# Retention feeding a WaveMLP block: the first half of a hand-written instruction order is written anew

## Chip, cores and metric

The kernel runs on one core of a Trainium2 chip. The metric is the time of one execution on the device in microseconds (us). All engines of a core run their own queues in order and wait for one another by semaphores: TensorE (PE), VectorE (DVE), ScalarE (ACT), GpSimd (POOL) and SyncE (SP). DMAs are issued from the queues of SyncE, ScalarE and GpSimd.

## What is computed

q, k and v have 4 batches, 8 heads, 768 steps and 64 channels. A retention with a decay per head gives x, and a gated mixing block follows on x.

```python
gamma = 1.0 - 2.0 ** (-5.0 - np.arange(H))
for t in range(S):                       # retention, scale = 1/8
    state = gamma * state + einsum('bhd,bhe->bhde', k[:, :, t], v[:, :, t])
    y[:, :, t] = scale * einsum('bhd,bhde->bhe', q[:, :, t], state)
x = y.transpose(0, 2, 1, 3).reshape(B, S, H * D)      # 4 x 768 x 512
theta = x @ w_theta
zr, zi = x * cos(theta), x * sin(theta)
u = x + einsum('ts,bsd->btd', w_tok_r, zr) + einsum('ts,bsd->btd', w_tok_i, zi)
out = u + maximum(u @ w_ch, 0.0)
```

## The kernel before

The retention is done in chunks. The work is cut into 24 *units*: unit n is one of 4 batches, one of 3 stretches of 256 steps, and one half of the heads (n even or odd). Two units of the same stretch make two blocks C of 128 steps of x; there are 24 blocks, six to a batch. Each step is a small function, and the table `ORDER` at the head of the file lists the calls of these functions one after the other. Each engine's queue gets its instructions in the order of that table; nothing reorders them afterwards. A token is a function, its arguments, and where it can run in several places, an engine: `s` SyncE's queue, `a` ScalarE, `v` VectorE, `p` GpSimd.

For unit n:

- `Lk`, `Lq`, `Lv` load 256 KB each of k, q and v (tiles `kqf`, `vf`).
- `ck` casts k to bf16 (tile `kqb`). q is cast either plainly (`cq`) or with its decay (`cqs`, a multiplication); after a plain cast the decay is put on at the end (`XA`, VectorE) instead of a plain copy (`XB`). `cv` casts v with its decay (tile `vb`).
- `Tk`, `Tq` transpose k and q on PE (four 128x128 each, into `kq_ps`), `E` copies them out (`kqT`). `Dk` does both by a DMA for some later units.
- `A` makes the scores (`at_ps`), `m` masks them (`at`, VectorE), `Y` multiplies them with v into `r_ps`.
- `ST` makes the unit's own state sum, `S0` and `S1` add the states up (`s`), `SB` casts them (`sbd`), and `I` adds the older state's share of the output.
- `XB` or `XA` gives the transposed output `xT`.

For block C: `Tx` and `Ex` (or `Dx`, a DMA) turn `xT` into `x_sb`; `Hh` multiplies `xT` with theta's weight (`th_ps`, four 512-wide matmuls); `CN` takes sine and cosine on ScalarE (`cs`); `z` multiplies them with x. The token weights come in rows: `Pw(r, g)` loads group g of the real (0) or imaginary (1) weight through GpSimd's queue; group 0 is row block 0, group 1 the blocks 1 and 2, group 2 the last three. `Tw` and `Ew` transpose a row block (six 128x128). `Pth` and `Pch` load the weights of theta and of the last product. `M(t, s)` is one of six pairs of 512-wide matmuls that make output block t; `u`, `Tu`/`Eu` or `Du`, `O`, `f`, `SO` finish and store it. `Z` is a filler: two 512-wide matmuls of zeros whose result nobody reads. There are 14 in the first half of the table and one at its end.

The constants: `const3` makes the small decays, `const9` and `const8` the large ones that `XA` needs (four activations each, `qx`), `const4` the identity, and `const7` loads ScalarE's table for the sine. DMAs on the two hardware queues share eight completion semaphores in turn, so one can be issued only when the eighth before it has landed.

Of the kernel before, what the change touches and what calls it, by code (L numbers as in the profile page):

```python
# [27 lines left out]
S0.2.v S1.2 SB.2.1.a Z.11 cqs.3.p Tq.3 Lv.3.s Tx.0 Tk.3 Z.3 ck.4.p Lv.4.s Lk.5.s Lq.5.s Lv.5.s
Lq.6.s Lk.6.s Lv.6.s Lq.7.s E.3.a SB.2.0.v I.2 Y.2 XB.2.1.a Ex.0.a cv.3.v cq.4.p Tk.4 Lq.8.s A.3
ST.3 Lk.7.s S0.3.v SB.3.0.a S1.3 Lv.7.s Lk.8.s Tx.1 Tq.4 SB.3.1.p cv.4.p m.3 Pw.1.0 XB.2.0.a Ex.1.a  # L30
I.3 Lv.8.s E.4.a cq.5.a Y.3 Pw.0.0 ST.4 Hh.0 ck.5.a S0.4.v XB.3.0.v XB.3.1.v cv.5.v CN.0.1 A.4
CN.0.0 Tq.5 Hh.1 Tk.5 SB.4.0.p SB.4.1.a Pw.0.1 Hh.2 m.4 E.5.v I.4 Y.4 ST.5 ck.6.a Tk.6 Tx.2 cq.6.a
CN.1.1 CN.1.0 XA.4.1 A.5 XA.4.0 m.5 Lq.9.s Ex.2.v S0.5.v z.0.p Tq.6 E.6.a CN.2.0 cv.6.p Hh.3
SB.5.0.v Tx.3 Tw.1.0 z.1.v SB.5.1.a Ew.1.0.v Ex.3.a CN.2.1 A.6 I.5 Y.5 ST.6 XA.5.0 z.2.v Tw.0.0
CN.3.0 Tx.4 CN.3.1 Ew.0.0.v S0.6.v XA.5.1 Ex.4.v Hh.4 CN.4.0 CN.4.1 Tw.0.1 M.0.1 Pw.1.1 z.3.v M.0.0
Tw.0.2 Pw.1.2 Ew.0.2.a SB.6.1.a Hh.5 z.4.p SB.6.0.p Lk.9.a M.0.3 ck.7.p cqs.7.p M.0.2 CN.5.1 CN.5.0
cq.8.a m.6 Ew.0.1.v Tw.1.1 Tw.1.2 Ew.1.1.v Lv.9.s M.0.4 M.1.0 Tx.5 Ew.1.2.v M.1.1 S1.6 Tk.7 M.1.4
Pch Ex.5.v z.5.v cv.7.v Tq.8 Tq.7 M.1.2 E.7.a M.0.5 I.6 Y.6 ST.7 A.7 ck.8.a u.0 S0.7.v m.7 XA.6.1
SB.7.1.a M.1.5 M.1.3 XA.6.0 Tw.1.3 M.2.5 Pw.0.2 M.2.3 u.1 S1.7 Tk.8 M.2.1 M.2.0 SB.7.0.v Ew.1.3.a
Tu.0 I.7 cv.8.p E.8.a cv.9.p Y.7 ST.8 A.8 cqs.9.v ck.9.v M.2.4 Du.1 Lk.10.s Eu.0.a XB.7.1.a XB.7.0.v  # L40
S0.8.v SB.8.0.v M.2.2 Tx.6 Tq.9 Tk.9 Lv.10.a cv.10.p ck.10.p Lq.10.s S1.8 u.2 m.8 O.0 E.9.a SB.8.1.a
Hh.6 Tw.1.4 I.8 Y.8 A.9 CN.6.0 Du.2 Lq.14.s CN.6.1 Ex.6.v f.0 ST.9 Tw.0.3 Hh.7 Ew.1.4.v Ew.0.3.a
S0.9.v Tw.0.4 M.3.0 Tw.1.5 CN.7.0 CN.7.1 M.3.2 Dx.7 M.3.1 M.3.5 M.3.3 Lv.12.s Lk.12.s Ew.1.5.v
XA.8.1 Ew.0.4.v Lq.12.s M.3.4 u.3 S1.9 Tw.0.5 Tk.10 M.4.5 cqs.10.p XA.8.0 m.9 M.4.3 Tq.10 SB.9.1.a
SB.9.0.a I.9 O.2 Lq.11.s Lk.11.s E.10.a Lk.15.s Ew.0.5.v Lk.14.s Y.9 ST.10 A.10 z.7.p Lv.11.s
# [12 lines left out]
SB.14.0.p Lv.16.s Hh.13 S1.14 u.8 Tx.12 M.10.1 cv.15.p cv.17.p SB.14.1.p M.10.0 M.10.4 cqs.18.v
M.10.5 CN.13.0 CN.13.1 Hh.12 CN.12.1 I.14 m.15 Y.14 CN.12.0 ST.15 S0.15.v XB.14.1.a SB.15.0.a M.10.3
cv.16.v Dk.16 Dk.17 Du.7 Dx.13 M.10.2 Dk.18 O.6 SB.15.1.p XB.14.0.v S1.15 I.15 Y.15 ST.16 SO.5.a  # L60
cv.18.p f.6 S0.16.v A.16 M.11.4 SB.16.1.p M.11.1 Lq.21.a Ex.12.a z.12.p SB.16.0.a Lk.19.s Lk.20.s
XB.15.0.a u.10 z.13.p XB.15.1.a m.16 O.7 Du.10 I.16 Y.16 ST.17 f.7 A.17 Tu.8 Hh.15 CN.15.1 CN.15.0
# [571 lines left out]
```

## Time and profile before

| | |
|---|---|
| time, three runs | 165.47, 165.74, 165.96 us; median 165.74 |
| span of the profiled execution, from its first to its last instruction | 164.0 us |
| PE busy | 153.7 us (94% of the span) |
| VectorE, ScalarE, GpSimd busy | 113.1, 79.6, 76.9 us |
| read from and written to HBM | 25.69 and 6.29 MB, 195 GB/s over the span |
| mean granted clock of TensorE | 0.999 |

The profiled execution's time with what lies around its span isn't given; the median of the three runs lies 1.74 us above the span. "Busy" is the time in which at least one instruction of the engine is under way, and matmuls overlap in their pipeline, so a busy PE isn't one that starts matmuls at its best rate. In the rows a name such as `kqb` is a tile's name without its buffer number, `x4` the number of instructions that a row gathers, and the brackets hold the engine's idle time before them with what ended it.

### The profile page before, as it was taken

To read this page: it belongs to the slowest core of one execution; us is meant where nothing else is said; L and a number is where in the kernel's file an instruction comes from. 1 tells how busy PE (TensorE), PEld (TensorE's weight loads), DVE (VectorE), ACT (ScalarE), POOL (GpSimd) and SP (SyncE) were. 2 spreads that over 40 slices of the span, in tenths; PEclk is the share of its full clock that TensorE was granted. 3 is DMA by queue.
4 is the path that set the end of the run, shared out by engine and by line. 5 is a ranking of instruction groups with operands and counts; after the bars stand their busy time and mean duration, and the time that the engine had idled before them with its cause. 6 is when DMAs were issued, how large, how long until landed. Compare 5 with 4: busy or idle time off the path is not lost.

```text
span 164.0 us, 4889 instructions
## 1 busy us (share of the span) xinstructions
PE 153.7 (94%) x2001; PEld 87.0 (53%) x2030; DVE 113.1 (69%) x210; ACT 79.6 (49%) x142; POOL 76.9 (47%) x109
## 2 busy tenths in 40 slices
PE   5997789999999999999999999999999999999992
PEld 1455556656666655654454565555555545455550
DVE  3298677977993896994879895789867760244462
ACT  4976889983658245762433725832341616000020
POOL 7957279186306733730307599951469104500000
PEclk9999999999999999999999999999999999999999
DMA  4999999999999999949999896999999438514455
GB/s 118 297 290 251 272 284 250 279 217 280 210 214 257 290 170 222 310 115 285 318 259 199 173 247 182 187 169 301 213 271 131 96 83 211 160 68 123 104 209 203
DMA packets 69062, 34.93 MB, mean 213 GB/s; under 512 B 26416, under 2 KB 66096, under 8 KB 69040
## 3 DMA queue, kind: packets, MB, share of 16 engines
q1 hardware_dynamic: 56032, 23.73, 67.4%
q10 hardware_dynamic: 10320, 7.47, 16.1%
q0 software_dynamic: 2688, 3.41, 12.1%
q8 instruction: 16, 0.26, 0.7%
q14 instruction: 6, 0.05, 0.1%
HBM read 25.69 MB, written 6.29 MB: 195 GB/s over the span
## 4 chain that ended last, share of the span: by engine, by line
PE 73%; DMA 12%; ACT 5%; POOL 4%; issue 2%; DVE 1%; DVEq 0%; SPq 0%; POOLq 0%; ACTq 0%
PE y_ps L509 35%; PE o_ps L536 12%; PE th_ps L469 9%; DMA row<-in_moe_w_tok_i_dram 5%; DMA kqf<-in_k_dram 4%; DMA kqf<-in_q_dram 4%; PE r_ps L423 3%; ACT qx L233 3%; PE at_ps L346 2%; PE r_ps L411 2%; PE kq_ps L316 2%; PE w_ps L491 2%; PE y_ps L561 2%; PE r_ps L373 1%; PE u_ps L521 1%
## 5 line engine op out<-in xcount | busy, mean ns | idle before, releaser
L509 PE MATMUL y_ps<-z,wti 128*128 128x512 bf16 x131 | 49.6, 379 | 1.0 <-issue 1.0
L509 PE MATMUL y_ps<-z,wtr 128*128 128x512 bf16 x131 | 49.7, 379 | 0.3
L483 POOL TENSOR_TENSOR z<-cs,x_sb 128x1024 bf16<-128x1024 bf16 x12 | 25.4, 2124 | 17.6 <-DMA x_sb<-xT 10.0
L355 DVE TENSOR_TENSOR at<-at_ps,mask 128x1024 bf16<-128x1024 f32 x24 | 29.2, 1216 | 0.6 <-PE at_ps L346 0.5
L308 POOL TENSOR_TENSOR vb<-vf,vsc 128x512 bf16<-128x512 f32 x17 | 18.0, 1063 | 21.3 <-DMA vf<-in_v_dram 21.0
L542 DVE SCALAR_TENSOR_TENSOR ot<-o_ps,u 128x512 f32<-128x512 f32 x23 | 15.8, 688 | 12.9 <-PE o_ps L536 12.8
L469 PE MATMUL th_ps<-wth,xT 128*128 128x512 bf16 x88 | 23.9, 379 | 0.5
L516 DVE TENSOR_TENSOR u<-y_ps,x_sb 128x512 bf16<-128x512 f32 x23 | 15.8, 688 | 12.0 <-PE y_ps L509 11.9
L536 PE MATMUL o_ps<-wch,uT 128*128 128x512 bf16 x88 | 23.2, 379 | 0.4 <-issue 0.2
L476 ACT ACTIVATE cs<-th_ps,zerob 128x512 bf16<-128x512 f32 x24 | 16.4, 684 | 12.7 <-PE th_ps L469 8.2
L476 ACT ACTIVATE cs<-th_ps,halfpi 128x512 bf16<-128x512 f32 x24 | 16.3, 684 | 10.5 <-issue 4.3
L139 POOL CAST sbd<-s 64x256 bf16<-64x256 f32 (+1 forms) x21 | 10.0, 476 | 22.9 <-DVE s L391 20.5
L509 PEld LDWEIGHTS <-wtr 128*128 128x128 bf16 x138 | 13.5, 98 | 12.7
L509 PEld LDWEIGHTS <-wti 128*128 128x128 bf16 x138 | 13.5, 98 | 11.9 <-DVE wti L139 0.2
L137 ACT COPY kqT<-kq_ps 128x1024 bf16<-128x1024 bf16 x12 | 12.1, 1012 | 10.9 <-PE kq_ps L316 10.9
L137 ACT CAST kqb<-kqf 128x512 bf16<-128x512 f32 x17 | 10.2, 619 | 8.0 <-DMA kqf<-in_k_dram 7.2
L469 PEld LDWEIGHTS <-xT 128*128 128x128 bf16 x96 | 8.9, 98 | 8.3
L536 PEld LDWEIGHTS <-uT 128*128 128x128 bf16 x92 | 8.4, 98 | 8.6
L316 PE MATMUL kq_ps<-ident,kqb 128*128 128x128 bf16 x120 | 11.2, 219 | 0.4 <-ACT kqb L137 0.2
L278 PE MATMUL zz<-zero 128*128 128x512 bf16 x27 | 9.5, 481 | 2.0 <-DVE zero L192 1.9
L423 PE MATMUL r_ps<-at,vb 64*64 64x128 bf16 x384 | 10.0, 221 | 1.1 <-DVE at L355 1.1
L316 PEld LDWEIGHTS <-kqb 128*128 128x128 bf16 x120 | 8.2, 98 | 4.5 <-POOL kqb L139 0.6
(77 smaller groups left out, 204.6 us busy)
## 6 DMA issues: line engine op xcount, KB each, us to landing
vf<-in_v_dram SPq DMA_DIRECT2D x20, 256.0 KB, 6.0
kqf<-in_k_dram SPq DMA_DIRECT2D x19, 256.0 KB, 5.3
kqf<-in_q_dram SPq DMA_DIRECT2D x17, 256.0 KB, 5.1
out_dram<-ot ACTq DMA_DIRECT2D x12, 256.0 KB, 3.0
out_dram<-ot SPq DMA_DIRECT2D x11, 256.0 KB, 3.1
kqf<-in_q_dram ACTq DMA_DIRECT2D x7, 256.0 KB, 5.4
kqf<-in_k_dram ACTq DMA_DIRECT2D x5, 256.0 KB, 5.0
vf<-in_v_dram ACTq DMA_DIRECT2D x4, 256.0 KB, 6.1
```

The lines of the kernel that those rows point to most:

```text
L137: nc.scalar.copy(dst, src)
L308: engines[e].tensor_mul(in_blocks(vb), by_token(raw["vf", n]), _bcast_last(K["vsc"][:, i, :, h * HU:(h + 1) * HU], D))
L316: nc.tensor.transpose(st["kq_ps", n][:, 4 * w + x, :], st["kqb", n][:, w, x * P:(x + 1) * P], K["ident"])
L355: nc.vector.tensor_mul(at.rearrange("p g j a t -> p (g j) (a t)"), st["at_ps", n].rearrange("p g j a t -> p (g j) (a t)"), _bcast_mid(K["m ...
L423: nc.tensor.matmul(st["R", n + 1][c][g * D:(g + 1) * D, j * P:(j + 1) * P], st["vb", n][rows, lo:lo + D], st["at", n][rows, g, j, a, :], s ...
L469: nc.tensor.matmul(th_ps, st["xT", C][:, j, :], K["wth"][:, j, :], start=(j == 0), stop=(j == 3))
L476: nc.scalar.activation(st["cs", C][:, w, :], st["th_ps", C], AF.Sin, bias=K["zerob" if w else "halfpi"], scale=1.0)
L483: engines[e].tensor_mul(st["z", b][:, c], st["cs", C], _bcast_mid(x_of(C), 2))
L509: nc.tensor.matmul(st["y", t], K["wT"][r][:, s0, t0 * P:(t0 + 1) * P], st["z", b][:, s0, r, :], start=(done == 0 and r == 0), stop=(done = ...
L516: nc.vector.tensor_add(st["u", t], st["y", t], st["x", b][:, t0, :])
L536: nc.tensor.matmul(o_ps, st["uT", t][:, j, :], K["wch"][:, j, :], start=(j == 0), stop=(j == nD - 1))
L542: nc.vector.scalar_tensor_tensor(st["ot", t], st["o", t], 0.0, st["u", t], ALU.max, ALU.add)
```

## The change

The first 435 of the table's 927 tokens are written in another order. From there on (at block 10's theta, about 68 us into the trace of before) the tables are equal but for one copy, `XB.12.1`, which goes from ScalarE to VectorE. The first half holds the same work: the same 49 loads of k, q and v, the same transposes, products and 14 fillers. What differs:

- the order of the loads, and their queues: 22 hardware DMAs of that half are on ScalarE's queue instead of 10;
- `Pth` stands behind the first state casts instead of behind unit 2's v cast; `Hh.0` and `Hh.1` stand ahead of `Y.3` and `ST.4`;
- five of the fillers stand ahead of `Tk.0` instead of seven;
- `cqs` on VectorE 5 times instead of 3, `cv` 4 instead of 3; `ck` on GpSimd 9 times instead of 5 and on VectorE once instead of 5; `E` on VectorE 6 times instead of 3; `Ew` on ScalarE 7 times instead of 3; `SB` on GpSimd 9 instead of 6;
- the units whose decay is put on at the end are 1, 5, 6, 7 and 8 instead of 4, 5, 6, 8 and 11.

```diff
 ORDER = """
-const2 Lv.0.s const1 const6.v Z.29 Z.2 const5 Z.38 Lk.0.a const3 Z.35 Z.8 Lq.0.s Lv.1.s Z.28 constA
-const4 Lq.1.a cqs.0.v const9 Lk.1.s cv.0.p Z.39 const8 ck.0.p Tk.0 Tq.0 ck.1.a E.0.v Lq.4.a ST.0
...
+const2 Lv.0.s const1 const6.v Z.29 Z.2 const5 Z.38 Lk.0.s constA Lk.1.a Lq.0.a Z.28 ck.0.p Z.8 const4 const3
+cqs.0.v ck.1.a Tk.0 cv.0.p Lv.2.s Lq.1.a Tq.0 Z.27 ST.0 Lv.1.s E.0.a const9 Lq.3.s Lk.3.a cv.2.p cq.1.p
...
```

The table is five lines shorter, so every line number of the kernel after is five lower (L303 for L308 and so on).

**ScalarE, the start of the program.** `kqf` are loads of k and q, `kqb` their casts, `kqT` the copy of the first transposes, `qx` the large decays, `xT` and `sbd` outputs and states. Before:

```order
L157 DMA kqf<-in_k_dram 128x4x128
L240 ACT_TABLE_LOAD
L240 ACTIVATE qsc<-arg,lscale 128x48
L240 ACTIVATE vsc<-arg,zerob 128x48
L157 DMA kqf<-in_q_dram 128x4x128
L233 ACTIVATE qx<-pos,lscale,lgp 128x512 x4
L233 ACTIVATE qx<-pos,lscale,lgp 128x256 x4
L137 CAST kqb<-kqf 128x512
```

Now:

```order
L152 DMA kqf<-in_k_dram 128x4x128
L152 DMA kqf<-in_q_dram 128x4x128
L235 ACT_TABLE_LOAD
L235 ACTIVATE qsc<-arg,lscale 128x48
L235 ACTIVATE vsc<-arg,zerob 128x48
L132 CAST kqb<-kqf 128x512
L152 DMA kqf<-in_q_dram 128x4x128
L132 COPY kqT<-kq_ps 128x1024
L228 ACTIVATE qx<-pos,lscale,lgp 128x512 x4
L152 DMA kqf<-in_k_dram 128x4x128
L152 DMA kqf<-in_q_dram 128x4x128
L152 DMA vf<-in_v_dram 128x4x128
```

The cast of unit 1's k and the copy E.0 have moved ahead of the decays, and the loads of q1, k3, q4 and v3 stand between these activations.

**GpSimd, up to theta's weight.** `ident` is the identity, `vb` a cast of v, `wth` theta's weight; the numbers tell tiles apart. Before:

```order
masks.py:199 AFFINE_SELECT ident_159<-ident_159 128x128
L308 TENSOR_TENSOR vb_174<-vf_91,vsc_131 128x512
L139 CAST kqb_166<-kqf_128 128x512
L302 TENSOR_TENSOR kqb_193<-kqf_164,qsc_130 128x512
L139 CAST sbd00_95<-s2_247 64x2x64
L308 TENSOR_TENSOR vb_253<-vf_143,vsc_131 128x512
L308 TENSOR_TENSOR vb_317<-vf_255,vsc_131 128x512
L173 DMA wth_99<-in_moe_w_theta_dram 128x4x512
L139 CAST kqb_406<-kqf_384 128x512
```

Now:

```order
L134 CAST kqb_148<-kqf_128 128x512
masks.py:197 MEMSET ident_153 128x128
masks.py:199 AFFINE_SELECT ident_153<-ident_153 128x128
L303 TENSOR_TENSOR vb_171<-vf_91,vsc_159 128x512
L303 TENSOR_TENSOR vb_214<-vf_173,vsc_159 128x512
L134 CAST kqb_164<-kqf_175 128x512
L134 CAST sbd00_95<-s2_221 64x2x64 x2
L168 DMA wth_99<-in_moe_w_theta_dram 128x4x512
L134 CAST kqb_310<-kqf_212 128x512
L134 CAST kqb_308<-kqf_290 128x512
```

The cast of k0 stands ahead of the identity; q1 is cast plainly here (`kqb_164`) and v1 no longer; behind the weight come k3 (`kqb_310`) and then k2 (`kqb_308`).

**ScalarE, the first sine and cosine.** `cs` are sine and cosine of a block. Before:

```order
L137 CAST kqb_581<-kqf_459 128x512
L137 CAST kqb_581<-kqf_457 128x512
L476 ACTIVATE cs_627<-th_ps_616,zerob_87 128x512
L476 ACTIVATE cs_627<-th_ps_616,halfpi_85 128x512
L137 CAST sbd00_95<-s2_427 64x4x64
```

Now:

```order
L132 COPY x_sb_560<-x_ps_473 128x512
L132 CAST kqb_568<-kqf_451 128x512
L471 ACTIVATE cs_585<-th_ps_546,halfpi_85 128x512
L471 ACTIVATE cs_585<-th_ps_546,zerob_87 128x512
L132 CAST xT_541<-r_ps_579 128x256
L471 ACTIVATE cs_660<-th_ps_563,zerob_87 128x512
L471 ACTIVATE cs_660<-th_ps_563,halfpi_85 128x512
```

Of unit 5 only q is cast here ahead of the first block's pair, and the second block's pair follows behind one copy (`xT_541`, unit 3's output).

More of the change, by code (lines that the diff above doesn't have):

```diff
@@ L28 @@
[L28 to L45, printed above, removed]
@@ L58 @@
[L58 to L62, printed above, removed]
-Dx.14 M.11.2 Tx.15 Lv.22.s SO.7.s M.11.0 M.11.5 S0.17.v SB.17.0.p M.11.3 XA.16.1 m.17 XA.16.0
@@ L86 @@
+Tuh.1 Euh.1 f.21 O.20 f.20 Oh.0 Oh.1 SO.21.a SO.22.s SO.20.s fh.0 SOh.0 fh.1 SOh.1 Z.31
 """.split()
```

92 lines of the change are left out of this document (55 added, 37 removed).

## The prediction

> **What bounds the kernel now.** I read the windows first, then the chain that ended last, then the timeline of the first 25 us. The windows give TensorE's (PE's) busy time in stretches of 8 us.
>
> ```profile
> 0.00:8.00 8.00, 6.01 (x22) 2.29 (x22) 2.34 (x7) 5.89 (x10) 6.64 (x35) 1.00 0.81 205
> 8.00:16.00 8.00, 6.87 (x162) 4.53 (x164) 6.97 (x13) 5.73 (x11) 5.35 (x8) 1.00 1.20 274
> 16.00:24.00 8.00, 6.51 (x141) 4.36 (x141) 5.49 (x13) 6.19 (x12) 4.68 (x8) 1.00 1.20 278
> 24.00:32.00 8.00, 7.71 (x152) 5.18 (x153) 6.72 (x14) 7.58 (x13) 4.59 (x4) 1.00 1.15 266
> 32.00:40.00 8.00, 7.77 (x66) 4.60 (x65) 6.02 (x13) 4.94 (x8) 5.40 (x6) 1.00 1.16 248
> ```
>
> PE idles 4.6 us before 24 us and 0.5 us in the next 16, while the DMA engines stay full (share over 1). The chain, in order of time, is PE alone from 35.68 us on.
>
> ```profile
> 9.27 6.62 DMA kqf<-in_k_dram
> ...
> 27.60 8.04 DMA row<-in_moe_w_tok_i_dram
> 35.68 0.84 PE w_ps L491 x12
> 36.53 0.86 PE y_ps L509 x4
> ...
> 40.12 0.35 PE r_ps L423 x16
> 40.59 0.23 PE at_ps L346 x16
> ...
> 47.61 0.86 PE th_ps L469 x4
> ...
> 72.39 0.22 PE kq_ps L316 x4
> ```
>
> So PE has a price for each group when nothing holds it: four transposes or small matmuls 0.22, six transposes 0.34, a theta block 0.86, a pair of 512-wide matmuls (a filler Z too) 0.43, A with Y 0.57, ST about 0.25. I keep an account: the start of a group minus the price of all groups in front of it on PE. It can't fall, since PE works in order. In front of 35.68 stand 14 filler pairs (6.0), the attention of units 0 to 5 and part of 6 with its transposes (9.7), six theta blocks (5.2), five x transposes (1.1), four row transposes (1.3) and four products (1.7): 25.0 us, so the account is 10.6. Counted on in the same way, 61.6 us stand in front of 72.39, which makes 10.8. All that the kernel loses on PE is lost by 36 us, and the change ends at about 68 us, behind which the work and its order are the same. The forecast is therefore the new account at the first products, less 10.6.
>
> The rows of the start, from the timeline of all engines:
>
> ```profile
> 1.67 1.28 ACT L240 ACT_TABLE_LOAD   x1 [1.67 <-DVE arg L217]
> 1.76 0.44 ACTq L157 DMA_DIRECT2D kqf<-in_q_dram  x1
> ...
> 1.92 5.48 PE L278 MATMUL zz<-zero 128*128 128x512 bf16 x14 [1.92 <-DVE zero L192]
> ...
> 2.96 0.33 ACT L240 ACTIVATE qsc<-arg,lscale 128x48 f32<-128x48 f32 x1
> ...
> 3.21 0.32 ACT L240 ACTIVATE vsc<-arg,zerob 128x48 f32<-128x48 f32 x1
> ...
> 3.96 4.89 ACT L233 ACTIVATE qx<-pos,lscale,lgp 128x512 f32<-128x512 f32 x8 [0.43 <-POOL lgp L228]
> ...
> 4.81 0.21 POOL masks.py:197 MEMSET ident<- 128x128 bf16 x1
> ...
> 5.09 0.29 POOL masks.py:199 TENSOR_SCALAR_AFFINE_SELECT ident<-ident 128x128 bf16<-128x128 bf16 x1
> ...
> 6.17 0.77 DVE L302 TENSOR_TENSOR kqb<-kqf,qsc 128x512 bf16<-128x512 f32 x1 [3.21 <-DMA kqf<-in_q_dram]
> ...
> 7.47 0.62 PE L316 MATMUL kq_ps<-ident,kqb 128*128 128x128 bf16 x8
> ...
> 8.13 0.69 DVE L139 COPY kqT<-kq_ps 128x1024 bf16<-128x1024 bf16 x1 [1.19 <-PE kq_ps L316]
> ...
> 8.87 0.42 PE L346 MATMUL at_ps<-kqT 64*64 64x128 bf16 x16
> ...
> 9.51 1.21 DVE L355 TENSOR_TENSOR at<-at_ps,mask 128x1024 bf16<-128x1024 f32 x1
> ...
> 10.61 1.01 ACT L137 COPY kqT<-kq_ps 128x1024 bf16<-128x1024 bf16 x1 [1.21 <-PE kq_ps L316]
> 10.64 0.68 DVE L302 TENSOR_TENSOR kqb<-kqf,qsc 128x512 bf16<-128x512 f32 x1
> ...
> 10.78 0.42 PE L423 MATMUL r_ps<-at,vb 64*64 64x128 bf16 x16 [0.20 <-DVE at L355]
> ...
> 12.45 0.42 PE L346 MATMUL at_ps<-kqT 64*64 64x128 bf16 x16
> ...
> 12.54 0.93 POOL L173 DMA_DIRECT2D wth<-in_moe_w_theta_dram  x1
> ...
> 13.47 0.62 POOL L139 CAST kqb<-kqf 128x512 bf16<-128x512 f32 x1
> ...
> 16.72 0.40 ACT L137 CAST sbd<-s 64x256 bf16<-64x256 f32 x1 [1.70 <-DVE s L391]
> ...
> 17.42 0.38 PE L411 MATMUL r_ps<-kqT,sbd 128*128 128x128 bf16 x4 [0.30 <-DVE sbd L139]
> ...
> 20.45 1.04 POOL L308 TENSOR_TENSOR vb<-vf,vsc 128x512 bf16<-128x512 f32 x1 [0.51 <-DMA vf<-in_v_dram]
> ...
> 21.79 1.04 PE L469 MATMUL th_ps<-wth,xT 128*128 128x512 bf16 x3
> ...
> 22.76 0.42 PE L346 MATMUL at_ps<-kqT 64*64 64x128 bf16 x16
> ```
>
> **The change part by part.** *Loads.* They land in the order of their issue. Of 256 KB loads the third, q0, released VectorE at 6.17, and the fourteenth, k4, landed at 15.9 (9.27 + 6.62): 0.89 us each. In the new order q1 is eighth, behind k1's cast on ScalarE, and lands at about 6.1 + 5 x 0.89 = 10.5; q2 follows at 11.4, k2 at 12.3, k3 at 13.2, q4 at 14.1, v3 at 15.0.
>
> *First transposes.* k0 is now second on SyncE's queue and shares with q0, so it lands near 6.5. GpSimd casts it (0.62) and only then makes the identity (4.81 to 5.38 before, 0.57): Tk.0 near 7.9, against 7.47. Five filler pairs stand ahead of it instead of seven, and two more stand behind it; E.0 is on ScalarE (1.01 for 0.69). A.0 comes at about 10.1, against 8.87, with equal work in front: 1.2 late.
>
> *Unit 1.* Its plain cast of q waits on GpSimd for q1 until 10.5 and ends at 11.1, where Tq.1 waits, with two fillers, Tk.1 and I.0 queued behind it on PE: Y.0 at 11.2 + 0.22 + 0.86 + 0.22 + 0.11 = 12.6, against 10.78. E.1 stands on VectorE behind two scaled casts (0.68 each), from m.0's end near 11.7: A.1 near 13.8, against 12.45.
>
> *Unit 2.* The cast of k3 now stands ahead of that of k2 on GpSimd; with k3 at 13.2 it costs little. The four shorter decays (eight take 4.89; I take 2.1 for these) stand on ScalarE ahead of E.3 (1.01) and SB.2 (0.40): from 14.6 to 18.1, so I.2 near 18.2, against 17.42. So far the change loses 0.8 to 1.4 us.
>
> *Theta ahead.* Here it gains. Before, PE has nothing past unit 3 until v4 lands: cv.4 runs at 20.45, A and ST of unit 4 follow, and theta's blocks come behind them, at 21.79 and after. Now Hh.0, Hh.1 and Tq.5 stand ahead of Y.3 and ST.4. They need the theta weight, which GpSimd issues at about 11.6 instead of 12.54.
>
> ```profile
> wth<-in_moe_w_theta_dram POOLq DMA_DIRECT2D x1, 512.0 KB, 6.8
> ```
>
> That makes 18.4, or up to 19.6 since it now shares the DMA engines with v3, k4 and v4 for longer. A.3 is done near 20.2, so Hh.0 starts at 20.3. A.4 is reached after Hh.0 0.86, Tx.1 0.22, Hh.1 0.86, Tq.5 0.22 and I.3 0.22: 22.7, as at 22.76 before. But 14.3 us stand in front of it now, against 13.7 (theta 0.86 and Tq.5 0.22 more, Y.3 0.22 and ST.4 0.25 less). The account there is 8.4 against 9.05.
>
> *Casts.* A scaled cast costs 1.04 on GpSimd and 0.68 on VectorE, a plain one 0.62 on GpSimd. Four casts of k go from VectorE to GpSimd and three of q leave ScalarE, while VectorE and ScalarE take over other copies; none is on the path but those named. I take 0, with 0.4 either way.
>
> *Token rows.* Their issue for blocks 1 and 2 of the imaginary weight moves from 27.60 to about 25.4. At 8.04 us from issue they land near 33.5; since the DMA engines have carried the same loads by then, up to 35.5 as before. PE needs them at about 36.0: covered, or 0.2 late.
>
> *The sum.* From A.4 to the first products the account grew by 1.55 before (9.05 to 10.6), the last 0.5 of it waiting for the row that landed at 35.64. I keep 1.6, since the product with the last block waits for z on VectorE, which stands behind z of two other blocks there. 8.4 + 1.6 = 10.0; less 10.6 is -0.6. Bounds of the growth: 0.9 without the row's wait and jitter, 2.6 if VectorE falls behind. The span becomes 164.0 - 0.6 = 163.4; the median of 165.74 lies 1.74 above the span that was profiled, which I carry over: **165.1 us**.
>
> **The clock**, first by the rows. In the windows of the fillers alone:
>
> ```profile
> 3.15:5.30 2.15, 2.15 (x6) 0.76 (x5) 1.00 1.17 327
> 6.56:7.42 0.86, 0.83 (x4) 0.20 (x2) 1.00 1.22 289
> ```
>
> Six start in 2.15 us (one in 0.43, as a row of 1.92 + 5.48 with 14 allows), then three in the last 0.86: PE doubled its pace 4.7 us after its first filler. The new order has fillers for only 1.92 to 5.75 and then leaves PE idle for about 2 us. [...]
>
> **The rivals.** *The early loss is all covered (chance 0.20).* The account is set by the row's landing at 35.6 alone, or by z there: 10.6 again, 165.7. For: DMA is full throughout. Against: the row waited only 0.5.
>
> *PE keeps half pace past its first transposes (0.20), slower.* Place: Tk.0 to A.1. At half pace the 2.3 us of work from 7.9 to A.0's end take 4.6. If the pace doubles by 10, 1.0 us is lost, half of it hidden behind q1 and the theta weight: about 165.6. It turns to slower where the pace doubles after 10.5: A.1 at 15.5, A.4 1.2 later, 166.3. For: the idle 2 us. Against: PE did hold full pace through idle 1.1 us in 8 to 16.
>
> *ScalarE's queue holds up the loads (0.16), slower.* k3, q4 and v3 stand behind E.0 and four decays there. If a DMA is issued only when the activations in front of it have run, k3 is issued near 11.8 instead of 8.7 and comes with the theta weight, at 16 or later; the casts of k2, q4 and v3 wait behind k3's on GpSimd, and I.2 goes to about 20.5. A.4's account is then near 10, the time 166.6. Against: at 1.76 a DMA left while two activations in front of it ran at 2.96 and 3.21. So the queue runs ahead by two at least; here five are needed. [...]
>
> **How the numbers follow.** Forecast 0.44, covered 0.20, half pace 0.20, queue 0.16. About 0.3%, 0.5 us, is what a measurement here can tell. Faster 0.44, same 0.20, slower 0.36. The growth's bounds, 0.9 and 2.6, put the forecast alone at 164.4 to 166.1; the slower rivals reach 166.3 and 166.6 with 0.3 more for chain steps that I can't see. Range 164.4 to 166.9.
>
> **What would show it.** Right: A.0 near 10.1, Tq.1 waiting for q1, theta's first block near 20.3 and ahead of ST.4, A.4 at 22.7, the row's wait gone. Wrong: fillers after Tk.0 0.43 apart, k3's issue after 10, a first theta block after 21.5, or a new PE wait of over 0.5 us between 36 and 68.

## Result and profile after

The changed kernel takes 167.07 us (median of 20 runs), the kernel before 165.72 beside it (20 runs), so 1.35 us more. Without the slow runs, those over 1.5% above the fastest of the same kernel (six of the changed kernel, the one profiled here among them, and one of before), the ratio is 1.0069, 95% interval 1.0051 to 1.0087: 0.7% slower. The runs of before lie within 0.6 us of one another but for one, those of the changed kernel between 165.4 and 168.4, but for one. The profile shown here is of a run of 168.19 us; a second one, of 167.46, is used for the account below.

The windows of the changed kernel, columns as in the prediction (PE's busy time behind the comma, with its instructions):

```profile
0.00:8.00 8.00, 4.47 (x11) 1.46 (x12) 2.26 (x7) 2.46 (x4) 4.97 (x34) 1.00 0.81 209
8.00:16.00 8.00, 7.16 (x114) 3.98 (x115) 5.11 (x9) 4.76 (x8) 7.04 (x9) 1.00 1.22 288
16.00:24.00 8.00, 7.43 (x148) 4.83 (x152) 6.69 (x13) 7.31 (x16) 5.88 (x10) 1.00 1.16 259
24.00:32.00 8.00, 7.55 (x186) 5.14 (x190) 7.83 (x16) 7.52 (x16) 5.47 (x7) 1.00 1.13 259
32.00:40.00 8.00, 7.04 (x96) 4.52 (x100) 6.96 (x14) 5.18 (x9) 3.56 (x5) 1.00 1.15 244
```

In 8 to 16 PE is busier than before (7.16 against 6.87 us) and does less: 114 matmuls instead of 162. Part of that is more wide fillers in this stretch (12 matmuls instead of 9), the rest a slower pace. In 32 to 40 it is less busy than before (7.04 against 7.77). The timeline shows both places and the start of theta:

```profile
1.92 4.45 PE L273 MATMUL zz<-zero 128*128 128x512 bf16 x10 [1.92 <-DVE zero L187]
...
7.98 1.01 PE L311 MATMUL kq_ps<-ident,kqb 128*128 128x128 bf16 x8 [1.61 <-POOL ident masks.py:199]
...
10.14 1.46 PE L273 MATMUL zz<-zero 128*128 128x512 bf16 x4
...
10.65 0.61 POOL L134 CAST kqb<-kqf 128x512 bf16<-128x512 f32 x1 [0.17 <-DMA kqf<-in_q_dram]
...
11.53 0.42 PE L341 MATMUL at_ps<-kqT 64*64 64x128 bf16 x16
11.79 0.93 POOL L168 DMA_DIRECT2D wth<-in_moe_w_theta_dram  x1
...
15.56 0.42 PE L341 MATMUL at_ps<-kqT 64*64 64x128 bf16 x16 [0.79 <-DVE kqT L134]
...
21.66 1.04 PE L464 MATMUL th_ps<-wth,xT 128*128 128x512 bf16 x3
...
24.16 0.42 PE L341 MATMUL at_ps<-kqT 64*64 64x128 bf16 x16
...
32.65 0.22 PE L450 MATMUL x_ps<-ident,xT 128*128 128x128 bf16 x1
33.77 0.34 PE L450 MATMUL x_ps<-ident,xT 128*128 128x128 bf16 x3 [0.91 <-issue]
```

Ten filler matmuls take 4.45 us and the first eight transposes 1.01, where eight took 0.62 before: half pace, and it lasts to 11.02, where the trace first records the full clock. Theta's first block starts at 21.66, and inside one group of four x transposes (Tx.4) PE stops for 0.91 us with nothing to wait for. The weight itself (its size and the time from issue to landing):

```profile
wth<-in_moe_w_theta_dram POOLq DMA_DIRECT2D x1, 512.0 KB, 8.6
```

Issued at 11.79, it lands at 20.4, not at 18.4. The table has the prediction's account (start of a group less the price of all groups in front of it) from the profiles; `changed` is the second profile, and the last two columns are experiments told below:

| at | before | forecast | changed | seven fillers ahead | seven, half weight |
|---|---|---|---|---|---|
| A.1 | 5.43 | 6.8 | 8.40 | 6.66 | 6.78 |
| I.2 | 6.93 | 7.7 | 9.12 | 7.38 | 7.49 |
| Hh.0 starts at | 21.79 | 20.3 | 21.51 | 21.11 | 19.88 |
| A.4 | 9.05 | 8.4 | 9.69 | 9.28 | 8.06 |
| first product of M.0 | 10.23 | 10.0 | 12.03 | 11.10 | 9.96 |
| 72 to 75 us | 10.8 | 10.2 | 12.63 | 11.83 | 10.75 |

The forecast set 10.0 at the first products against 10.6 before; carried on with the 0.2 that before loses behind them, that is 10.2. Of the 2.4 us between 10.2 and 12.63, 1.3 are lost up to A.4, 0.7 between it and the first products, and 0.4 behind those.

### The profile page after: what moved, and what is told of

Read it like the earlier page. It is cut to its first block, busy times and chain, and to the rows that moved or that the text cites. A ratio compares the mean times of both kernels' runs of the same rounds, so it can differ in the third digit from the quotient of the medians.

```text
span 166.5 us, 4890 instructions
## 1 busy us (share of the span) xinstructions
PE 154.3 (93%) x2000; PEld 86.4 (52%) x2030; DVE 113.6 (68%) x203; ACT 79.1 (48%) x144; POOL 78.8 (47%) x114
## 3 DMA queue, kind: packets, MB, share of 16 engines
q0 software_dynamic: 2688, 3.41, 12.6%
## 4 chain that ended last, share of the span: by engine, by line
PE 74%; DMA 12%; DVE 5%; issue 3%; ACT 2%; POOL 1%; DVEq 0%; SPq 0%; ACTq 0%; POOLq 0%
PE y_ps L504 30%; PE th_ps L464 11%; PE o_ps L531 11%; DMA kqf<-in_k_dram 8%; DMA kqT<-kqb 4%; PE r_ps L418 4%; PE kq_ps L311 3%; PE at_ps L341 3%; PE r_ps L406 3%; PE w_ps L486 2%; PE y_ps L556 2%; PE r_ps L368 2%; PE x_ps L450 2%; DVE at L350 1%; PE zz L273 1%
## 5 line engine op out<-in xcount | busy, mean ns | idle before, releaser
L537 DVE SCALAR_TENSOR_TENSOR ot<-o_ps,u 128x512 f32<-128x512 f32 x23 | 15.9, 690 | 15.6 <-PE o_ps L531 15.5
L134 POOL CAST sbd<-s 64x256 bf16<-64x256 f32 (+1 forms) x24 | 10.8, 451 | 29.2 <-DVE s L386 17.8
L303 POOL TENSOR_TENSOR vb<-vf,vsc 128x512 bf16<-128x512 f32 x16 | 17.1, 1074 | 11.5 <-DMA vf<-in_v_dram 11.3
L134 POOL CAST kqb<-kqf 128x512 bf16<-128x512 f32 x17 | 11.5, 693 | 9.5 <-PE kq_ps L311 5.7
L311 PE MATMUL kq_ps<-ident,kqb 128*128 128x128 bf16 x120 | 11.1, 226 | 2.0 <-POOL ident masks.py:199 1.6
L132 ACT CAST kqb<-kqf 128x512 bf16<-128x512 f32 x14 | 8.6, 622 | 8.1 <-DMA kqf<-in_k_dram 8.1
L273 PE MATMUL zz<-zero 128*128 128x512 bf16 x27 | 10.3, 511 | 2.0 <-DVE zero L187 1.9
L132 ACT COPY kqT<-kq_ps 128x1024 bf16<-128x1024 bf16 x9 | 9.1, 1010 | 5.6 <-PE kq_ps L311 5.6
```

Of the source, the lines that this page charges most:

```text
L132: nc.scalar.copy(dst, src)
L134: engines[e].tensor_copy(dst, src)
L303: engines[e].tensor_mul(in_blocks(vb), by_token(raw["vf", n]), _bcast_last(K["vsc"][:, i, :, h * HU:(h + 1) * HU], D))
L311: nc.tensor.transpose(st["kq_ps", n][:, 4 * w + x, :], st["kqb", n][:, w, x * P:(x + 1) * P], K["ident"])
L537: nc.vector.scalar_tensor_tensor(st["ot", t], st["o", t], 0.0, st["u", t], ALU.max, ALU.add)
```

## Experiments

Each ratio is to the kernel before on the same chip, with its 95% interval. Names of tokens and tiles are those of the kernels; "seven ahead" stands for the second experiment's kernel.

**1. The changed kernel again.**

> The changed kernel as it is, run again for its spread and a second profile. Theory (PE's pace is released in windows of about 3.4 us that run freely, and the idle time between the fifth filler pair and Tk.0 spoils most of them): runs spread from 165.4 to 168.4 us, median near 167.0, and the profile's release of the clock, its 0.43 us fillers and its A.4 move together: each 1 us of later release costs at most 1 us of A.4. Rival (the loss is a fixed one: casts on GpSimd, the theta weight, the stop inside Tx.4): the same account in front of A.4, 9.8 us, and in front of 75 us, 12.6, whatever the release.

Measured: 167.49 us (166.71 to 167.82), ratio 1.0093 (1.0070 to 1.0116). The trace records changes of the granted clock only at multiples of 3.41 us from one another (here 5.26, 8.67 and 12.08). The windows of this grid, with the granted clock in the third column from the end:

```profile
1.85:5.26 3.41, 3.34 (x8) 1.19 (x9) 1.10 (x5) 1.99 (x4) 2.45 (x13) 1.00 0.90 245
5.26:8.67 3.41, 1.41 (x13) 0.73 (x11) 0.69 (x1) 0.61 (x2) 2.17 (x4) 1.00 1.22 290
8.67:12.08 3.41, 3.41 (x42) 1.49 (x41) 1.41 (x4) 3.41 (x5) 3.16 (x6) 0.50 1.22 290
```

Here the clock is released at 5.26 after a window full of fillers, the next window holds the idle time, and the third runs at half. In the first profile the release came only at 11.02. (Before its first release the column reads 1.00 though the pace is half, as in the first row.) There the grid cut the 4.45 us of fillers in two, and neither half released the clock:

```profile
0.78:4.19 3.41, 2.27 (x6) 0.89 (x7) 1.57 (x6) 1.84 (x3) 2.94 (x22) 1.00 0.54 158
4.19:7.61 3.42, 2.18 (x6) 0.56 (x4) 0.53 (x1) 0.62 (x1) 1.42 (x8) 1.00 1.21 299
```

A.4's account is 9.84 in the first profile and 9.69 in the second, with A.1 at 8.55 and 8.40. So the half pace is there in both, by two ways. But what is lost behind A.4 is the same in both, 2.9 to 3.0 by 75 us: part of the rival holds too. A window lost after a release lowers a run's mean clock to 0.990 or less: 8 of the 20 runs of the result and 5 of these 6 show that, and none of the 12 with seven ahead. A late release doesn't show in that mean, so how many of the other runs had one isn't known.

**2 and 3. Where the fillers stand.**

```diff
# 2: the changed kernel with seven fillers ahead of Tk.0
-... Z.28 ck.0.p Z.8 const4 ...      ... S1.0 Z.18 SB.0.1.p Pth Z.11 Tk.1 ...
+... Z.28 ck.0.p Z.8 Z.18 Z.11 const4 ...      ... S1.0 SB.0.1.p Pth Tk.1 ...
# 3: the kernel before with five
-... Lv.1.s Z.28 constA ...      ... cv.0.p Z.39 const8 ...      ... m.0 Tk.1 ...
+... Lv.1.s constA ...      ... cv.0.p const8 ...      ... m.0 Z.28 Z.39 Tk.1 ...
```

> The changed kernel with the two filler pairs that stand between Tq.1 and Tk.1 put ahead of Tk.0: seven there, as in the kernel before, still fourteen in all. Theory (the half pace is the loss): the clock is released by 8.7 us, the spread of the runs shrinks to about 0.6 us, A.4 starts near 22.8, and the median falls to 165.1 to 165.6. Rival (the loss lies elsewhere in the new order): median stays within 0.4 us of the changed kernel's 167.0.

> The kernel before with only five filler pairs ahead of Tk.0; the other two stand between Tq.1 and Tk.1, as in the change. Nothing else moves. Theory: PE idles from about 6.3 to 7.5 us, the release is late in most runs, the spread grows to 1 us or more, and the median is 0.4 to 1.2 us above the kernel before. Rival (fillers play no part): within 0.2 us of the kernel before, with its spread of 0.6.

Measured: the third 166.06 us, ratio 1.0032 (1.0011 to 1.0052), in two groups: seven runs at 165.63 to 166.07 and five at 166.84 to 167.06. The two groups are 1.1 us apart, and only fillers have moved. The profiled run is one of the five, and it has lost a window of the clock:

```profile
1.32:4.74 3.42, 2.82 (x7) 1.03 (x8) 1.57 (x6) 2.63 (x5) 2.90 (x18) 1.00 0.69 193
4.74:8.15 3.41, 1.57 (x28) 0.78 (x26) 0.83 (x2) 3.41 (x7) 3.28 (x6) 1.00 1.22 290
8.15:11.56 3.41, 3.19 (x42) 1.71 (x39) 2.90 (x6) 1.24 (x3) 1.63 (x4) 0.50 1.22 290
```

So I read the groups as the half pace, which comes or not with the phase of the windows and costs about 1 us when it comes. That is shown for the profiled run alone: the mean clock of the other four, 0.997 to 0.999, has no lost window, and a late release wouldn't show in it. The seven others, without the loss, still lie 0.2 to 0.3 us above before, probably because the two pairs now run among other work instead of in PE's idle time.

The second kernel contradicts my theory: 166.85 us, ratio 1.0068 (1.0044 to 1.0091), hardly less than the change, though its clock is released at 4.75 and stays. Nor did the spread shrink to 0.6 us, as expected: the runs go from 165.85 to 168.31, none with a lost window, so most of the spread has another cause, which stays open. The reason for the median is in one row:

```profile
21.11 1.04 PE L464 MATMUL th_ps<-wth,xT 128*128 128x512 bf16 x3 [1.27 <-DMA wth<-in_moe_w_theta_dram]
```

With the pace right PE is at theta's first block 1.27 us early, and waits for the weight, which lands at 21.0 (9.4 us from issue here). The half pace had been hidden behind this landing, or the landing behind the half pace.

**4. Theta's first blocks put back behind Y.3 and ST.4, seven ahead.**

```diff
-... SB.3.0.p Hh.0 Lv.6.a Tx.1 S1.3 Ex.0.a Ex.1.v Hh.1 ... Tq.5 Pw.0.0 I.3 CN.0.0 CN.0.1 Pw.0.1 A.4 Y.3 ck.5.p ST.4 cv.5.v ...
+... SB.3.0.p Lv.6.a Tx.1 S1.3 Ex.0.a Ex.1.v ... Pw.0.0 I.3 Pw.0.1 Y.3 ck.5.p ST.4 Hh.0 cv.5.v ... CN.0.0 CN.0.1 A.4 Tq.5 Hh.1 m.4 ...
```

> The changed kernel with seven filler pairs ahead of Tk.0, and with theta's first two blocks put back behind Y.3 and ST.4, where they stood before. It tells what the early theta blocks are worth once the pace is right. Theory of the prediction (PE would idle there for v4): 0.4 to 0.7 us slower than the kernel that has seven ahead and the early theta. Rival (PE has enough other work, or the theta weight lands too late to help): within 0.2 us of it.

Measured: 167.89 us, ratio 1.0116 (1.0087 to 1.0146), so 0.8 to 1.0 us slower than with theta ahead, the intervals just touching. PE waits there for what it had covered:

```profile
20.63 0.40 PE L450 MATMUL x_ps<-ident,xT 128*128 128x128 bf16 x4 [0.77 <-DVE kqT L134]
21.96 0.27 PE L406 MATMUL r_ps<-kqT,sbd 128*128 128x128 bf16 x2 [0.72 <-DVE s L390]
```

That isn't the forecast's gain, though. Five of the six runs (167.70 to 168.40) have a mean clock of 0.987 to 0.990, so about one window at half pace, and the sixth, the profiled one, kept its clock and took 166.52, less than the median of seven ahead. Its window around these waits came near to losing the clock too:

```profile
20.04:23.46 3.42, 2.05 (x43) 1.23 (x44) 2.26 (x5) 2.10 (x5) 2.59 (x5) 1.00 1.21 290
```

So theta ahead is worth 0.8 to 1.0 us here, most of it probably because it keeps PE busy and with it the clock; where the five runs lost their window isn't shown, and one run with the clock kept can't size the forecast's gain.

**5, 6, 11 and 13. The stop in Tx.4.** PE's program of some 4,030 loads and matmuls is read by DMA in pieces (queue and kind, then packets, MB, share of the DMA engines' time):

```profile
q8 instruction: 16, 0.26, 0.7%
```

0.26 MB in 16 pieces is 16 KB each, and each holds about 126 pairs of a load and a matmul; 128 fits all that follows. Of the eight profiles of the new order with 2,048 loads, five stop for 0.9 us or more ahead of weight load 482, and the fourth for 0.5; the seventh and fifteenth, which lose time elsewhere before it, don't. Counted back by 128, the earlier ends are at loads 354, 226 and 98. By the packets of that queue, PE enters the piece that ends at 482 at 27.40 in the changed kernel; the next piece is read at 31.35 to 32.51, with the DMA engines full (share 1.15 from 30.8 to 33.9), and PE has come to the end of its piece at 32.59. It goes on at 33.77. Before, PE enters at 25.81, the read ends at 30.41, and PE passes at 31.55 without a stop, 1.14 after it.

```diff
# 5: seven ahead, each filler pair as ten small matmuls: 112 more weight loads in front
-        for _ in range(2):
-            nc.tensor.matmul(t, K["zero"][:, :P], K["zero"], ...)
+        for _ in range(10):
+            nc.tensor.matmul(t[:64, :104], K["zero"][:, :64], K["zero"][:, :104], ...)
# 6: before, six pairs as four of 256 columns: 12 more loads
+        w = 256 if n in (15, 27, 34, 18, 23, 11) else 512
+        for c in range(1024 // w):
+            nc.tensor.matmul(t[:, :w], K["zero"][:, :P], K["zero"][:, :w], ...)
# 11: seven ahead, without Z.3 and Z.39, and one matmul in five other pairs: 9 fewer
+        for _ in range(1 if n in (27, 34, 23, 35, 15) else 2):
# 13: seven ahead, as 6 but with 11 pairs: 22 more loads
+        w = 512 if n in (29, 2, 38, 31) else 256
```

> The kernel with seven fillers ahead of Tk.0, with each filler pair cut into ten matmuls of 104 columns on 64 rows in place of two of 512 (about the same time, zeros as before): 112 more weight loads stand in front of everything else on PE. Theory (PE stops inside Tx.4 because it comes to the end of a 16 KB piece of its instructions, load 482, before the next piece, asked for when PE entered the piece before, has been read behind the other DMAs): the ends move 112 loads forward, to places 7.5 us or more apart, the stop of 0.65 us in Tx.4 is gone and no other of over 0.3 us without a releaser comes before 68 us; account at 73 us 11.0 to 11.3 against 11.8, median 0.4 to 0.8 us under that with two matmuls each. Rival (the stop belongs to Tx.4 itself: its tile, or a wait that the trace does not show): the stop stays in Tx.4, time as before the edit within 0.3.

> The kernel before with six of its filler pairs cut into four matmuls of 256 columns each: 12 more weight loads in front, the same filler time. It brings the end of the third piece of instructions to load 470 of the old count, which PE reaches 4.7 us after it entered that piece, against 5.5. Theory of the pieces: a stop of 0.6 to 1.3 us without a releaser appears near 30.5 to 32, part of it given back at the row's wait at 35.7; account at 72 us 11.1 to 11.6 against 10.8, median 166.1 to 166.6. Rival (the pieces play no part): no stop, 165.7 within 0.2.

> The kernel with seven fillers ahead of Tk.0 and nine filler matmuls fewer behind it: Z.3 and Z.39 out, one matmul instead of two in five others, where PE waits anyway. It brings the end of the third piece of instructions nine loads later, into Tw.0.2, which PE reaches some 0.85 us after Tx.4. Theory of the pieces: the stop of 0.65 us in Tx.4 is gone or under 0.3, nothing else changes, the account (by the work that is left) ends 0.3 to 0.6 us lower at 73 us, median 0.3 to 0.7 us under that with all fillers. Rival (the stop stays where it is, or the fillers' idle time lowers the clock again): no faster.

> The kernel with seven fillers ahead of Tk.0, with eleven of its filler pairs cut into four matmuls of 256 columns: 22 more weight loads in front at the same filler time, and 2070 in all, so no 17th piece. The end of the third piece moves to a place that PE reaches 6.5 us after it entered it, where it needed 6.1. Theory of the pieces: no stop of over 0.3 us without a releaser before 68 us, account at 73 us 11.1 to 11.5 against 11.8, median 0.3 to 0.7 us under that without the cut. Rival (time won there is lost at the next wait): stop gone, account at 73 us within 0.2 of 11.8.

Measured: the stop moves with the count. In 5, 11 and 13 Tx.4 runs through; in the fifth kernel's timeline, for one:

```profile
32.82 0.39 PE L450 MATMUL x_ps<-ident,xT 128*128 128x128 bf16 x4
33.05 1.03 PE L464 MATMUL th_ps<-wth,xT 128*128 128x512 bf16 x4
```

That rules out the rival that the stop belongs to Tx.4. The time didn't follow: 168.10 (ratio 1.0136), 166.95 (1.0053) and 167.06 (1.0076), none faster than seven ahead beyond the intervals. Two reasons are probably the edits' own costs. The fifth kernel has 2,168 loads and a 17th piece, which is read at 161.5 to 162.4, while the last stores run: PE's last matmuls end near 162, as with seven ahead, but the span is 166.8 instead of 165.2; that this read delays the stores isn't shown apart. The eleventh lost the clock where its fillers were missing:

```profile
9.62:13.03 3.41, 1.79 (x60) 1.25 (x59) 3.16 (x6) 2.75 (x4) 3.17 (x5) 1.00 1.22 290
13.03:16.44 3.41, 3.08 (x52) 2.25 (x48) 2.37 (x5) 3.18 (x8) 3.22 (x5) 0.50 1.24 281
```

The thirteenth has neither, and its account is 10.7 at M.0's first product against 11.1, but 11.73 at 73 us against 11.83: won and lost again, as its rival said (where, the eighteenth tells). The sixth, the opposite test, took 166.22 us, ratio 1.0025 (1.0011 to 1.0039), but its profile shows no stop (PE passed 1.13 us after the read's end) and a clock released at 7.70 instead of 6.57: it decides nothing.

**7, 8, 15 and 16. The weight's landing, by moving issues.**

```diff
# 7: seven ahead, Pth behind cv.0 (8: and the ten-matmul fillers of 5)
-... Tk.0 cv.0.p Lv.2.s ...      ... SB.0.1.p Pth Tk.1 ...
+... Tk.0 cv.0.p Pth Lv.2.s ...      ... SB.0.1.p Tk.1 ...
# 15: seven ahead, v4 on ScalarE's queue (16: and the cut fillers of 13)
-... const8 ck.2.p Lk.5.a ...      ... XA.1.1 Lv.4.s Lq.5.s ...
+... const8 ck.2.p Lv.4.a Lk.5.a ...      ... XA.1.1 Lq.5.s ...
```

> The kernel with seven fillers ahead of Tk.0, with the theta weight's DMA issued right behind cv.0 on GpSimd, near 9 us instead of 11.6. Theory (the early theta blocks wait 1.27 us for that weight, which lands 9.4 us after its issue because more loads run beside it than before): it lands near 18.5, Hh.0 starts at 19.9 to 20.3 instead of 21.1, A.4 near 22.7; up to 0.5 us is taken back by the casts of k2, k3 and q4, whose loads share with it; median 0.3 to 0.9 us lower. Rival (other loads are delayed by as much): Hh.0 no earlier than 20.8, the median within 0.3 us.

> Both edits together: cut fillers and the theta weight's early issue. Theory (three causes that add up: half pace, the weight's landing, the piece of instructions): account at 73 us 10.2 to 10.8, median 165.0 to 165.8, at or under the kernel before. Rival (a later wait, such as for the row of the last block at 35 us, takes back what is won): account at 73 us 11.2 or more.

> The kernel with seven fillers ahead of Tk.0, with v4's load taken from SyncE's queue and issued by ScalarE behind the second four decays, near 14.2 us as in the kernel before, instead of 10.9. Theory (the theta weight's packets begin only when the loads issued before them are through, 15.7 us with k4 and v4 in front against 14.9 before): the weight lands 0.6 to 1.3 us earlier, Hh.0 at 19.9 to 20.5, A.4's account 8.2 to 8.7, median 0.3 to 0.8 us lower. Rival (v4 itself is then late, and ST.4 or the casts behind it on GpSimd wait): A.4 no earlier, or the same time.

> The cut of e13 and the later v4 together, and the whole weight. Theory (half pace, landing and stop are the three causes): account at 73 us 10.2 to 10.9, median 165.1 to 165.8, at or below the kernel before. Rival (the rows' landing or z then holds PE): 166 or more.

Measured: 168.85 (ratio 1.0189), 170.34 (1.0283), 168.06 (1.0134) and 168.02 us (1.0126): all slower. The weight does land earlier in 15 (8.5 us from issue, 9.4 with seven ahead), and theta starts at 20.09 with 0.33 of wait. But the load put behind is then the late one, and GpSimd works in order:

```profile
21.48 1.04 POOL L303 TENSOR_TENSOR vb<-vf,vsc 128x512 bf16<-128x512 f32 x1 [3.72 <-DMA vf<-in_v_dram]
...
23.07 1.15 POOL L134 CAST sbd<-s 64x256 bf16<-64x256 f32 x2
```

v4's cast waits 3.72 us for its load, the state casts for unit 3 stand behind it, and PE's I.3 waits 1.8 for those. In 7 it is v3 that GpSimd waits for (3.93), and I.2 on PE (2.99); that wait left 1.09 us of work in a window, and the clock was half in the next, 21.83 to 25.25, so part of the loss in 7 is the clock's. The rivals hold: the DMA engines are full (share 1.21 from 18.42 to 21.83 in 7), and one landing is bought with another.

**9 and 10. Theta ahead on the kernel before.**

```diff
# 9
-... Tq.4 SB.3.1.p ...      ... ST.4 Hh.0 ck.5.a ...      ... Tq.5 Hh.1 Tk.5 ...
+... Tq.4 Hh.0 Hh.1 SB.3.1.p ...      ... ST.4 ck.5.a ...      ... Tq.5 Tk.5 ...
# 10: and
-... M.0.1 Pw.1.1 z.3.v ...
+... S0.5.v Pw.1.1 z.0.p ...
```

> The kernel before, with nothing changed but theta's first two blocks put ahead of I.3, right behind Tq.4. The theta weight lands at 19.3 us there, so they start at 19.5 to 20 in place of 21.79 and 23.34, and fill PE's waits for v4. Theory (what the early theta blocks win is taken back where PE next waits: for the row that lands at 35.64, and for the third 16 KB piece of instructions): A.4 at 22.0 to 22.4 with an account of 7.6 to 8.2 against 9.05, yet 10.5 to 10.9 at 72 us and a median within 0.3 us of the kernel before. Rival (the step of the prediction: the growth behind A.4 is kept): 0.6 us or more faster, about 165.0.

> The same, with the issue of the row for blocks 1 and 2 of the imaginary weight put ahead of z.0 on GpSimd, near 26 us instead of 27.6. Theory: the row lands 1 to 1.6 us earlier, the wait at Tw.1.1 is gone, and what is left is the piece of instructions: account at 72 us 9.9 to 10.4, median 165.1 to 165.5. Rival (z.0 comes later by the issue and the products wait for it, or the row lands no earlier among the other loads): 165.5 to 166.0.

Measured: the ninth 165.87 us, ratio 0.9988 (0.9969 to 1.0008), no change. A.4's account falls to 7.69, and at 72 us it is 10.99. So the gain is taken back, as the theory said, but not by the row or the piece: no row is waited for, and the first loss behind is another.

```profile
24.44 1.02 PE L469 MATMUL th_ps<-wth,xT 128*128 128x512 bf16 x3 [0.76 <-ACT cs L476]
```

Block 2's theta waits 0.76 us for a PSUM bank (the kernel has two for `th_ps`) that ScalarE's cosine of block 0 frees. The tenth, 167.00 us (ratio 1.0072), is slower than its own profile (166.02, its fastest run) explains; why stays open.

**12, 14, 17 and 18. The weight's landing and the half pace, apart.** Half of the weight is loaded and used for both halves, in the kernel with seven ahead (12), in the change as it is with five (14), in the kernel before (17), and with seven ahead and the cut fillers of 13 (18).

```diff
-        nc.gpsimd.dma_start(out=K["wth"], in_=moe_w_theta.rearrange("(a p) e -> p a e", p=P))
+        nc.gpsimd.dma_start(out=K["wth"][:, :2], in_=moe_w_theta[:2 * P].rearrange("(a p) e -> p a e", p=P))
-            nc.tensor.matmul(th_ps, st["xT", C][:, j, :], K["wth"][:, j, :],
+            nc.tensor.matmul(th_ps, st["xT", C][:, j, :], K["wth"][:, j % 2, :],
```

> The kernel with seven fillers ahead of Tk.0, but only the first half of theta's weight is loaded, and used for both halves, so its output is another; PE's work is the same. The weight's landing, 21.0 us with the whole, comes some 3 to 4 us sooner. Theory (with the half pace gone, the weight's landing holds A.4 back): Hh.0 at 19.8 to 20.1 without a wait, A.4 at 22.3, its account 8.0 against 9.28; behind it up to all of this is lost again in the piece of instructions and for the rows: median 0.3 to 1.0 us under that with the whole weight. Rival (another wait stands right behind: xT or v4): A.4 no earlier than 23.2, median the same.

> The changed kernel as it is, five fillers ahead of Tk.0, but with only the first half of theta's weight loaded and used twice (another output, the same work on PE). With seven fillers this won 1.1 us. Theory (two limits side by side: at half pace PE itself reaches theta's blocks only at 21.5, after the whole weight has landed): it wins little here, median 166.4 to 167.0, with Hh.0 near 21.3 and A.4's account over 9.3 in a profile whose clock is released after 10. Rival (the weight's landing is the whole loss): 165.7, as with seven fillers.

> The kernel before, with only the first half of theta's weight loaded and used twice (another output, the same work on PE). There PE does not wait for the weight: it lands at 19.3 and the first block starts at 21.79. Theory (what the half weight won with seven fillers was its landing): no change here, 165.5 to 165.9. Rival (the 256 KB spared let every later load land sooner, and that is the gain): 0.5 us or more faster, 165.2 or less.

> Seven fillers ahead of Tk.0, half of theta's weight loaded and used twice (another output, the same work on PE), and eleven filler pairs cut into four matmuls of 256 columns, which moves the end of the third piece of instructions 22 loads forward. Without the cut: 165.73, a stop of 1.15 us in Tx.4, account 10.75 at 72 us. Theory (the stop is on the path once the pace and the weight are cured): account 9.8 to 10.3, median 165.0 to 165.4. Rival (what is won at the stop is lost at the next wait, as with the whole weight): 165.6 to 165.9.

| fillers ahead of Tk.0 | whole weight | half weight |
|---|---|---|
| seven | 1.0068 (1.0044 to 1.0091) | 0.9993 (0.9975 to 1.0011) |
| five (the change) | 1.0069 (1.0051 to 1.0087) and 1.0093 (1.0070 to 1.0116) | 1.0088 (1.0057 to 1.0120) |
| the kernel before | 1 | 0.9975 (0.9956 to 0.9994) |

By this table the loss up to A.4 has two causes side by side. Curing one of the two gives nothing that the intervals tell from noise; curing both gives 0.75%, 1.2 us. With both cured, theta starts on time (twelfth kernel):

```profile
19.88 1.04 PE L464 MATMUL th_ps<-wth,xT 128*128 128x512 bf16 x3
```

The cell with five fillers and half the weight isn't pure half pace. The profiled run of the fourteenth, its fastest (166.31), had its clock released at 6.75 and kept it:

```profile
20.20 1.04 PE L464 MATMUL th_ps<-wth,xT 128*128 128x512 bf16 x3
```

Its account at A.4 is 8.38, 0.3 over the twelfth's 8.06, and it took 0.6 us more than the twelfth's median. So part of what five fillers cost, 0.3 to 0.6 us by this one run, isn't the pace; probably it is the two pairs themselves, which no longer run in PE's idle time.

The last line of the table corrects the size: half a weight is 256 KB less for the full DMA engines, and that alone is worth 0.4 us where nobody waits for the weight. About 0.8 of the 1.2 us are left for its landing, with some 0.6 us either way by the intervals. My theory for that run (no change) was wrong.

The eighteenth adds the moved stop and gives 165.83 us, ratio 1.0003 (0.9982 to 1.0025), no gain over the twelfth. Its account is still 8.96 at 35 us, 1.6 under before's 10.6, and 10.91 at 72: PE loses 1.4 of that at 60 us, for the cast of k11.

```profile
59.94 0.62 ACT L132 CAST kqb<-kqf 128x512 bf16<-128x512 f32 x1 [1.54 <-DMA kqf<-in_k_dram]
...
60.62 0.40 PE L312 MATMUL kq_ps<-ident,kqb 128*128 128x128 bf16 x4 [1.38 <-ACT kqb L132]
```

In the twelfth, with the stop, the same cast starts at 59.78 and waits 0.36 for its load. The load of k11 comes at nearly the same time in both, so the stop of 0.9 us is paid out of that wait. For the same cast PE waits 0.41 us in the fifth and 0.44 in the thirteenth, and not at all with seven ahead, so part of what they won was lost there too.

## Why the prediction was wrong

*What bounds.* Right in the main: what is lost on PE is lost by the first products, but for 0.6 to 0.9 us (12.03 to 12.63 in the second profile; before, 0.2 behind its 10.6).

*Loads, first transposes.* Right: q1 released GpSimd's cast at 10.65 (10.5 forecast), Tk.0 waited for the identity, 7.98 (7.9). A.0 came at 11.53, not 10.1. With seven ahead, at full pace, the steps come as forecast: A.0 at 10.05 (10.1), A.1 at 13.67 (13.8), I.2 at 17.87 (18.2).

*The clock: the step that failed first.* I had the half-pace rival with A.1 at 15.5 and A.4 1.2 later, and gave it 0.20; measured 15.56 and 24.16, 1.4 later. The forecast's own path ran its first transposes at full pace. I argued against it that PE had kept full pace through 1.1 us of idle time in 8 to 16. That row says nothing on a release: in these runs it took a fuller window to get the clock than to keep it (2.82 us of PE and more got it, 1.95 kept it; below). In the third kernel the lost clock's window is 8.15 to 11.56, one of 3.41 us. And the grid doesn't lie at one place in all profiles: it has an edge at 0.78 us in the first, at 1.85 in the second and at 1.32 in the third kernel's, and with the same five pairs ahead the clock was released at 11.02 in the first and at 5.26 in the second.

*Theta ahead: the term that was mis-sized.* The gain at A.4 is there: with the landing and the pace cured its account was 8.06, against 8.4 forecast, and on the kernel before it fell from 9.05 to 7.69 (experiment 9). But I set the weight at 18.4 to 19.6, from 6.8 us after issue with something added for sharing. It landed at 20.4 to 21.0. By the packets, its first one came 1.4 us after the end of the issue before and 2.8 to 3.1 us after it in the new order, when k4 and v4, issued ahead of it, were all but through (91 of their 512 KB were left in the changed kernel); in the kernel before v4 was issued later than the weight. I had followed each load's own queue, and not which loads stand in front of the weight on the shared engines.

*Growth behind A.4.* 1.6 forecast to the first products, bounds 0.9 and 2.6; measured 2.3 (9.69 to 12.03), inside the bounds, and 2.9 by 75 us. 1.1 of it is the stop between two pieces of PE's program, which no row of before showed. With it gone, most of the time won was lost again at the load of k11 (experiments 13 and 18).

*Covered (0.20).* True in part, at another place. Neither the row nor z took the gain back, but theta's PSUM bank (experiment 9) and the load of k11 at 60 us (18). Even with the pace and the landing cured, nothing is left of the 0.6 us that were forecast: with half the weight in both, the new order has 0.9993 and the old one 0.9975, the intervals overlapping.

*ScalarE's queue (0.16).* It did not hold up the loads, as I had weighed it. In the changed kernel's timeline, from E.0 on:

```profile
9.03 1.01 ACT L132 COPY kqT<-kq_ps 128x1024 bf16<-128x1024 bf16 x1 [3.21 <-PE kq_ps L311]
9.04 0.37 ACTq L152 DMA_DIRECT2D kqf<-in_k_dram  x1
9.45 0.53 ACTq L152 DMA_DIRECT2D kqf<-in_q_dram  x1
...
9.94 0.82 ACT L228 ACTIVATE qx<-pos,lscale,lgp 128x512 f32<-128x512 f32 x1
10.02 0.52 ACTq L152 DMA_DIRECT2D vf<-in_v_dram  x1
...
10.65 2.22 ACT L228 ACTIVATE qx<-pos,lscale,lgp 128x512 f32<-128x512 f32 x3
```

The loads stand behind E.0 and four decays. Two were issued while E.0 ran, before the first decay, and the third while the first decay ran: at 9.04 five instructions ahead of the load were unfinished, so the queue ran ahead by five entries at least, where the trace of before had shown two.

*Token rows.* Right: covered, no wait for a row in the changed kernel. The casts' term, 0, wasn't measured apart.

The median, 167.07, lies above the whole of the likeliest case (164.4 to 166.1) and 0.17 above the range's end. No one of the slower rivals gives it: the half pace was forecast alone and at 166.3, and came together with the late weight and the stop.

## What to carry to other kernels

When an edit gains in one place, write down what each later stage would wait for next, and when that lands: here the pace, a weight's landing and a load at 60 us stood so close behind one another that curing the first or the second alone showed nothing. Two causes side by side are told apart only by a table of both cured, one cured and none. And count fillers or other early work by the clock's window that they must fill (here 2.82 of 3.41 us released it and 2.38 did not), not by their number: moving two of fourteen cost about 1 us, in some runs only.
